# The tails of token mixing in two column tiles of TensorE instead of zero-padded weights

## The chip, the cores and the metric

The kernel runs on one core of one Trainium2 chip. The metric is the device time of one execution in microseconds (us), from five runs shown as their median, lowest and highest. A separate profiler record of one execution gives the trace. TensorE is called PE here, its weight loads PEld, VectorE DVE, ScalarE ACT, GpSimd POOL, and SyncE (which only issues transfers here) SP.

## The reference

A pooling attention feeds an MLP mixer. Sizes: 8 batches, 8 heads, 576 tokens, head width 64, so a model width of 512.

```
k_p, v_p = mean of k, v over groups of 8 tokens          # 72 pooled keys
attn     = softmax(q @ k_p.T / 8)                         # 576 x 72 a head
x        = heads of (attn @ v_p) side by side             # 576 x 512 a batch
A        = relu(x.T @ w_tok1)                             # 512 x 256
u        = x + (A @ w_tok2).T                             # token mixing, second stage
out      = u + relu(u @ w_ch1) @ w_ch2                    # channel mixing, 1536 wide
```

The change is in the second stage of token mixing, `u = x + (A @ w_tok2).T`: 256 hidden values are contracted into 576 tokens by 512 columns.

## The kernel before

**Tiling of the tokens.** A batch has 576 tokens, which is four blocks of 128 and one of 64. The block of 64 is called the tail. Two batches (2p and 2p+1) share one tail tile of 128 partitions: the even batch has partitions 0 to 63, the odd one 64 to 127. That holds for the attention's output (`xt`) and for the mixed tail (`u_tails[:, p, :]`), so four pairs make four tail blocks, and channel mixing treats these as a ninth unit of work (n = 8) after the eight batches.

**The stage that is changed.** Line 400, `u(c)`, is the second stage of token mixing for block c. For c below 4 it is two matmuls into one accumulator of `ps_one` (a pool of three accumulator banks, line 60), one for each half of the 256 hidden values. `AT` holds the 256 hidden values on partitions, in two halves m. For c = 4, called `u4`, the block belongs to two batches with different `AT`, kept in `tails[pair, half]` (line 389). The weights of the tail tokens, `w_tok2[:, m, 512:576]`, have 64 columns. They are copied into `w_tok2t`, a tile of 128 columns for each half: for the even batch the weights are in columns 0 to 63 and the rest is zero, and for the odd batch the other way round. So four full matmuls of 128 x 128 x 512 accumulate into the same 128 x 512 accumulator. The zero columns add nothing to the other batch's rows. One DVE addition (line 411) then adds `xt` and writes `u_tails`.

**Building the padded weights.** Line 614 clears `w_tok2t` on DVE at the start. Lines 129 and 130, at the end of `permute_tok2`, copy the weights into their places with two POOL instructions. Lines 127 and 128 permute `w_tok2` itself, on POOL as well. On POOL's queue the two copies stand ahead of the loads of batch 1's q and v and of `w_ch2`, and of batch 2's k and q.

**The order of work.** The schedule is written by hand: every engine does its instructions in the order in which the program emits them. `unit(n, at)` (line 590) runs the channel mixing of unit n: for each of 12 hidden blocks four matmuls (line 512) and a ReLU on ACT (line 516), then the second layer (line 534) and the stores. Between steps of it, the tables `FIRST` to `LATER` (lines 559 to 576) name steps of the next batch to be emitted (of batch n itself with `<`, of batch n+2 with `>`): attention scores (`s`, line 253), attention times values (`av`, line 344), first token mixing (`at`, line 395), second (`u`, line 410), transposes of u (`t`, line 420, with the copy at line 421), or spilling u to memory and reading it back in transposed blocks (`M`, `T`). `u4` occurs four times, for the odd batches: in unit 0 as "t1 u4 u3", in unit 2 as "u2 t0", "u4", "t1" at successive places, and in units 4 and 6 as "u0 u2 u4" at one place. The transposes `t` share a single accumulator (`pt`), so a `t` waits until the DVE copy of the one before has emptied it.

**Row tiles.** `score4` (line 253) already divides PE: its matmuls contract over 32 partitions only, and four of them, with `tile_position=(l * 32, 0)`, sit in four row groups of the array. All other matmuls of the kernel use the array whole.

Of the kernel before, what the change touches and what calls it, by code (L numbers as in the profile page):

```python
# [9 lines left out]
BF16 = mybir.dt.bfloat16  # L10
# [10 lines left out]
def kernel(  # L21
# [14 lines left out]
    nc = tc.nc  # L36
    B, H, S, D = q.shape
    P = 128
    POOL = 8
    SP = S // POOL  # L40
    BP, BR = 64, S // 64
# [10 lines left out]
    singles = ctx.enter_context(tc.tile_pool(name="singles", bufs=1))  # L52
# [11 lines left out]
    ident = singles.tile([P, P], BF16)  # L64
    w_tok1 = singles.tile([P, 6, DT], BF16)
    w_tok2 = singles.tile([P, 2, S], BF16)
    w_tok2t = singles.tile([P, 2, 2, P], BF16)
    w_ch1 = singles.tile([P, 4, DC], BF16)
    w_ch2 = singles.tile([P, NM, DM], BF16)
    f2 = singles.tile([P, 2, S], BF16)  # L70
# [35 lines left out]
    def q_pairs(a0, a1):  # L106
        return q[0, 2 * a0:2 * a1].rearrange("(a l) (p r) d -> (l p) a (r d)", l=2, r=BR)

    def load(key, b):
        if b < B:  # L110
            load_q(b) if key == "q" else load_kv(b, k if key == "k" else v, key)

    def load_tok():
        nc.gpsimd.dma_start(out=f2, in_=moe_w_tok2.rearrange("(c p) n -> p c n", p=P))
        w = moe_w_tok1.rearrange("(p r) n -> p r n", r=BR)
        for half in range(2):
            rows = slice(half * BP, (half + 1) * BP)
            nc.gpsimd.dma_start(out=w_tok1[rows, 0:4, :],
                                in_=w[:, 0:8, :].rearrange("p (c u) n -> p c u n", u=2)[:, :, half])
        for half in range(2):  # L120
            rows = slice(half * BP, (half + 1) * BP)
            nc.gpsimd.dma_start(out=w_tok1[rows, 4 + half, :], in_=w[:, 8, :])

    def permute_tok2():
        src = f2.rearrange("t m (p r) -> t m r p", r=BR)
        dst = w_tok2.rearrange("t m (r p) -> t m r p", p=BP)
        for m in range(2):
            nc.gpsimd.tensor_copy(out=dst[:, m], in_=src[:, m])
        for half in range(2):
            nc.gpsimd.tensor_copy(out=w_tok2t[:, :, half, half * BP:(half + 1) * BP], in_=w_tok2[:, :, 8 * BP:S])  # L130

    def load_ch1():
        for g in range(3):
            cols = slice(g * 512, (g + 1) * 512)
            nc.gpsimd.dma_start(out=w_ch1[:, :, cols], in_=moe_w_ch1[:, cols].rearrange("(p c) n -> p c n", c=4))

    def load_ch2(gs):
        for g in gs:
            nc.gpsimd.dma_start(out=w_ch2[:, 4 * g:4 * g + 4, :],
                                in_=moe_w_ch2[g * 512:(g + 1) * 512, :].rearrange("(c p) n -> p c n", p=P))  # L140
# [13 lines left out]
    tails = {}  # L154

    def batch_steps(b):

        par, first = b % 2, b == 0
        st = {}
# [16 lines left out]
        def late(key):  # L176
            if key not in st:
                pool, shape = {"x": (mix, [P, 4, DM]), "u": (mix, [P, 4, DM]), "uT": (mix, [P, 4, 4 * P]),
                               "AT": (att, [P, 2, DM]), "qD": (att, [P, 2, 2, S])}[key]
                st[key] = pool.tile(shape, BF16, name=key)  # L180
            return st[key]
# [218 lines left out]
        def u(c):  # L400
            def go():
                ps = ps_one.tile([P, 512], FP32, name="p1")
                if c < 4:
                    mms = [(w_tok2[:, m, c * P:(c + 1) * P], st["AT"][:, m, :]) for m in range(2)]
                    dst, x = late("u")[:, c, :], st["x"][:, c, :]
                else:
                    mms = [(w_tok2t[:, m, half, :], tails[b // 2, half][:, m, :]) for half in range(2) for m in range(2)]
                    dst, x = u_tails[:, b // 2, :], st["xt"]
                for i, (w, a) in enumerate(mms):
                    nc.tensor.matmul(out=ps, lhsT=w, rhs=a, start=(i == 0), stop=(i == len(mms) - 1))  # L410
                nc.vector.tensor_tensor(out=dst, in0=ps, in1=x, op=ALU.add)  # L411
            return go

# [165 lines left out]
    def head(s):  # L579
        if s[0] == "d":  # L580
            ps = ps_tr.tile([P, 512], FP32, name="pt")
            for _ in range(int(s[1:])):
                nc.tensor.matmul(out=ps, lhsT=warm[:, 0:P], rhs=warm, start=True, stop=True)
        elif s[0] == "c":
            a = int(s[1:])
            (nc.vector.tensor_copy if a % 2 else nc.scalar.copy)(out=loaded[0, "q"][:, a, 0:BR * D], in_=qf[:, a, :])
        else:
            batches[0][1][s]()

    def unit(n, at):  # L590
        if n + 2 < B:
            batches[n + 2][0]()
        for i, _ in enumerate(unit_steps(n, batches[n][2] if n < B else None)):
            for s in at.get(i, "").split():
                if s[0] == "l":
                    load(s[1], n + int(s[2]))
                    continue
                ahead = {"<": 0, ">": 2}.get(s[0], 1)
                s = s.lstrip("<>")
                if n + ahead < B and ((n + ahead) % 2 or s not in ("u4", "t4", "M4", "T4")):  # L600
                    batches[n + ahead][1][s]()

    with tc.manual_schedule(engines={PE, POOLE, DVE, ACT, SYNC}):
        batches = [batch_steps(b) for b in range(B)]
        nc.vector.memset(warm, 0.0)
        for a in range(2):
            nc.sync.dma_start(out=qf[:, a:a + 1, :], in_=q_pairs(a, a + 1))
        load("k", 0)
        make_identity(nc, ident)
        load("q", 0)  # L610
        load("v", 0)
        nc.vector.memset(kpz, 0.0)
        nc.vector.memset(w_tok1[:, 4:6, :], 0.0)
        nc.vector.memset(w_tok2t, 0.0)
        load_tok()
        load_ch1()
        load("k", 1)
        permute_tok2()
        load("q", 1)
        load("v", 1)  # L620
        load_ch2((0, 1, 2))
        batches[0][0]()
        for s in HEAD.split():
            head(s)
        load("k", 2)
        load("q", 2)
        batches[1][0]()
        unit(0, FIRST)
        unit(1, SECOND)
        unit(2, THIRD)  # L630
        unit(3, FOURTH)
        for n in range(4, B + 1):
            unit(n, LATER)
# [30 lines left out]
```

The softmax here doesn't subtract the row's maximum and nothing guards it: scores larger than these inputs give would overflow.

## Time and profile before

| what | value |
|---|---|
| median of five runs | 275.58 us (274.8 to 275.73) |
| profiled execution | 274.8 us |
| its span, first to last instruction | 273.0 us |
| mean granted clock of TensorE | 0.997 |
| PE busy | 264.3 us (97%) |
| DVE, ACT, POOL busy | 141.8, 110.4, 131.1 us |
| matmuls of `u4` | 16, first at 51.5 us, last at 208.8 us |

The times of matmuls need care. Matmuls are pipelined: the trace gives a 128x512 matmul 379 ns from start to end, but the next one starts before this one ends. What a matmul takes from PE's time is the distance between starts. The table of waits names the engine that released a waiting instruction; the chain of work that ended last follows the program back from its last instruction, and gives each piece the time that it added.

### The profile page before, as it was taken

What the parts mean: (1) busy time and instruction counts of PE and PEld (TensorE: products, weight loads), DVE (VectorE), ACT (ScalarE), POOL (GpSimd) and SP (SyncE); (2) the same over time, 40 slices, a digit from 0 to 9 for tenths busy, and PEclk for the clock granted to TensorE, in tenths of its full rate; (3) what the DMA queues carried; (4) which work ended last, traced back from release to release, by engine and by line L of the source; (5) the groups of instructions that cost most, each with busy time, mean ns of one, the idle gap of its engine ahead of it and who ended that gap; (6) DMA issues with size and microseconds to landing.
All of it is one profiled execution on the core that took longest, in us unless ns stands there. A gap on an engine that the chain in (4) does not pass through costs nothing.

```text
span 273.0 us, 4513 instructions
## 1 busy us (share of the span) xinstructions
PE 264.3 (97%) x1801; PEld 130.5 (48%) x1832; DVE 141.8 (52%) x280; ACT 110.4 (40%) x182; POOL 131.1 (48%) x121
## 2 busy tenths in 40 slices
PE   8999999999999999999999999999999999999994
PEld 3874444545453544444444444544454444444443
DVE  5586777763583676466267627662665061022022
ACT  2443780058207534425632483147413603703600
POOL 8695223999998990899099999300000000000000
PEclk9999999999999999999999999999999999999998
DMA  8999999990997910994399363224223624024024
GB/s 165 191 202 208 204 205 202 226 189 5 176 133 126 214 29 5 147 221 123 77 158 221 110 119 73 59 66 115 57 61 96 129 62 99 0 56 100 2 48 106
DMA packets 36838, 32.68 MB, mean 120 GB/s; under 512 B 14289, under 2 KB 30289, under 8 KB 36817
## 3 DMA queue, kind: packets, MB, share of 16 engines
q0 software_dynamic: 18672, 17.64, 41.0%
q1 hardware_dynamic: 17984, 14.62, 21.0%
q8 instruction: 14, 0.23, 0.3%
q10 hardware_dynamic: 160, 0.13, 0.2%
q14 instruction: 8, 0.06, 0.1%
HBM read 38.21 MB, written 11.80 MB: 183 GB/s over the span
## 4 chain that ended last, share of the span: by engine, by line
PE 89%; ACT 3%; DVE 2%; DMA 2%; issue 1%; POOL 0%; POOLq 0%
PE p L512 32%; PE p L534 32%; PE p L410 6%; PE p L395 6%; PE p L344 3%; PE p L260 3%; ACT ex L265 2%; DMA kr<-in_k_dram 2%; PE pt L420 1%; ACT GT L516 1%; PE p L226 1%; PE p L546 1%; PE p L204 1%; PE pt L376 1%; PE p L461 0%
## 5 line engine op out<-in xcount | busy, mean ns | idle before, releaser
L534 PE MATMUL p<-w_ch,GT 128*128 128x512 bf16 x404 | 98.9, 379 | 0.9 <-issue 0.3
L516 ACT ACTIVATE GT<-p 128x512 bf16<-128x512 f32 x108 | 63.8, 598 | 70.4 <-PE p L512 69.5
L512 PE MATMUL p<-uT,w_ch 128*128 128x512 bf16 x371 | 91.3, 379 | 0.7
L512 PEld LDWEIGHTS <-w_ch 128*128 128x128 bf16 x432 | 40.5, 98 | 47.5 <-issue 2.7
L534 PEld LDWEIGHTS <-GT 128*128 128x128 bf16 x420 | 38.0, 98 | 42.0 <-issue 3.3
L520 DVE TENSOR_TENSOR o<-p,u 128x512 f32<-128x512 f32 x32 | 21.9, 684 | 31.2 <-PE p L534 31.0
L265 ACT ACTIVATE ex<-p 72x1024 bf16<-72x1024 f32 (+1 forms) x42 | 31.7, 807 | 13.4 <-PE p L260 13.4
L147 POOL TENSOR_TENSOR t<-t 72x512 f32<-72x512 f32 x24 | 30.3, 1264 | 1.9
L411 DVE TENSOR_TENSOR u<-p,x 128x512 bf16<-128x512 f32 x32 | 21.7, 690 | 14.7 <-PE p L410 14.4
L146 POOL TENSOR_TENSOR t<-kr 72x1024 f32<-72x1024 bf16 x12 | 25.5, 2122 | 7.2 <-DMA kr<-in_k_dram 6.5
L146 POOL TENSOR_TENSOR t<-vr 72x1024 f32<-72x1024 bf16 x12 | 25.5, 2124 | 0.8
L442 DVE STREAM_TRANSPOSE uT<-v 128x512 bf16<-128x512 bf16 x16 | 10.4, 688 | 24.0 <-DMA v<-mem 24.0
L248 DVE STREAM_TRANSPOSE qD<-qb 128x576 bf16<-128x576 bf16 x28 | 20.5, 794 | 0.4 <-DMA qb<-in_q_dram 0.4
L362 DVE TENSOR_TENSOR x<-p,den 128x512 bf16<-128x512 f32 x28 | 19.4, 691 | 1.0
L410 PE MATMUL p<-AT,w_tok 128*128 128x512 bf16 x64 | 18.4, 379 | 0.2 <-ACT GT L516 0.2
L386 ACT ACTIVATE AT<-p 128x512 bf16<-128x512 f32 x7 | 4.2, 597 | 32.2 <-PE p L395 32.2
L344 PEld LDWEIGHTS <-ex 72*128 72x128 bf16 x280 | 13.0, 98 | 7.9 <-DVE x L362 0.7
L356 DVE RECIPROCAL den<-p 128x8 f32<-128x8 f32 (+1 forms) x35 | 7.1, 202 | 15.8 <-PE p L344 15.3
L395 PE MATMUL p<-x,w_tok 128*128 128x512 bf16 x56 | 14.5, 379 | 0.1
L344 PE MATMUL p<-vp,ex 72*128 72x65 bf16 x280 | 14.1, 193 | 0.4 <-ACT ex L265 0.4
L104 POOL DMA_DIRECT2D qb<-in_q_dram x7 | 5.2, 738 | 18.1 <-DVE qD L248 14.1
L260 PE MATMUL p<-qD,kD 32*72 32x512 bf16 (+1 forms) x224 | 11.3, 294 | 0.2
(105 smaller groups left out, 205.8 us busy)
## 6 DMA issues: line engine op xcount, KB each, us to landing
out_dram<-o SPq DMA_DIRECT2D x70, 128.0 KB, 2.4
kr<-in_k_dram POOLq DMA_DIRECT2D x7, 576.0 KB, 13.9
qb<-in_q_dram POOLq DMA_DIRECT2D x7, 576.0 KB, 6.3
vr<-in_v_dram POOLq DMA_DIRECT2D x7, 576.0 KB, 14.5
w_ch<-in_moe_w_ch_dram POOLq DMA_DIRECT2D x6, 512.0 KB, 13.4
mem<-u SPq DMA_DIRECT2D x8, 256.0 KB, 2.1
v<-mem SPq DMA_DIRECT2D x8, 160.0 KB, 3.7
v<-mem SPq DMA_DIRECT2D x8, 128.0 KB, 3.2
```

The lines of the kernel that those rows point to most:

```text
L146: eng.tensor_tensor(out=t4[:, 0:n], in0=t[:, hs, 0:4], in1=t[:, hs, 4:8], op=ALU.add)
L147: eng.tensor_tensor(out=t4[:, 0:n, 0:2], in0=t4[:, 0:n, 0:2], in1=t4[:, 0:n, 2:4], op=ALU.add)
L248: nc.vector.transpose(out=late("qD")[:, g, db].rearrange("m (r j u) -> m u r j", u=2, r=BR), in_=st["qraw"][:, g].rearrange("m (u r d) -> ...
L265: nc.scalar.activation(out=exv[:, a, :, gs.start:gs.stop, n0:n0 + n], in_=pss[a][0:SP, :, 0:len(gs) * n].rearrange("j l (g n) -> j l g n", ...
L344: nc.tensor.matmul(out=halves[h // 4][:, (h % 4) * (D + 1):(h % 4 + 1) * (D + 1)], lhsT=st["ex"][:, h * S + n0:h * S + n0 + P], rhs=st["vp ...
L395: nc.tensor.matmul(out=ps, lhsT=w_tok1[:, c if c < 4 else 4 + par, m * P:(m + 1) * P], rhs=st["x"][:, c, :] if c < 4 else st["xt"], start= ...
L410: nc.tensor.matmul(out=ps, lhsT=w, rhs=a, start=(i == 0), stop=(i == len(mms) - 1))
L411: nc.vector.tensor_tensor(out=dst, in0=ps, in1=x, op=ALU.add)
L512: nc.tensor.matmul(out=ps, lhsT=w_ch1[:, kk, m * P:(m + 1) * P], rhs=uT[:, kk, :], start=(kk == 0), stop=(kk == 3))
L516: nc.scalar.activation(out=GT[:, m, :], in_=ps, func=AF.Relu)
L520: nc.vector.tensor_tensor(out=o_sb, in0=ps, in1=(u_tails if n == B else st["u"])[:, c, :], op=ALU.add)
L534: nc.tensor.matmul(out=pss[c], lhsT=GT[:, m, c * P:(c + 1) * P], rhs=w_ch2[:, m, :], start=(m == 0), stop=(m == NM - 1))
```

## The change

The second stage of token mixing for the tails uses the 64 tail columns of `w_tok2` directly, and puts the two batches into two column tiles of the array, each 64 columns wide. The even batch's matmuls write partitions 0 to 63 of the accumulator and have `tile_position` (0, 0); the odd batch's write partitions 64 to 127 and have (0, 64). Their order changes from half by half to alternating halves, so that matmuls of different column tiles follow one another. There are four matmuls and four weight loads in a `u4`, as before; each load has 64 columns instead of 128. The tile `w_tok2t`, the DVE instruction that clears it and the two POOL copies that fill it are gone. The addition into `u_tails` is as it was.

```diff
-    w_tok2t = singles.tile([P, 2, 2, P], BF16)
...
         for m in range(2):
             nc.gpsimd.tensor_copy(out=dst[:, m], in_=src[:, m])
-        for half in range(2):
-            nc.gpsimd.tensor_copy(out=w_tok2t[:, :, half, half * BP:(half + 1) * BP], in_=w_tok2[:, :, 8 * BP:S])
...
                 if c < 4:
-                    mms = [(w_tok2[:, m, c * P:(c + 1) * P], st["AT"][:, m, :]) for m in range(2)]
                     dst, x = late("u")[:, c, :], st["x"][:, c, :]
+                    for m in range(2):
+                        nc.tensor.matmul(out=ps, lhsT=w_tok2[:, m, c * P:(c + 1) * P], rhs=st["AT"][:, m, :],
+                                         start=(m == 0), stop=(m == 1))
                 else:
-                    mms = [(w_tok2t[:, m, half, :], tails[b // 2, half][:, m, :]) for half in range(2) for m in range(2)]
                     dst, x = u_tails[:, b // 2, :], st["xt"]
-                for i, (w, a) in enumerate(mms):
-                    nc.tensor.matmul(out=ps, lhsT=w, rhs=a, start=(i == 0), stop=(i == len(mms) - 1))
+                    for m in range(2):
+                        for half in range(2):
+                            nc.tensor.matmul(out=ps[half * BP:(half + 1) * BP], lhsT=w_tok2[:, m, 8 * BP:S],
+                                             rhs=tails[b // 2, half][:, m, :], start=(m == 0), stop=(m == 1),
+                                             tile_position=(0, half * BP))
                 nc.vector.tensor_tensor(out=dst, in0=ps, in1=x, op=ALU.add)
...
-        nc.vector.memset(w_tok2t, 0.0)
```

## The prediction

> **What bounds the kernel now.** I read the page's busy times first, then the chain that ended last, then the groups of instructions, and after these the timeline of the four places where `u4` stands. From the page, the busy time of each engine with its share of the span, and the chain's shares by engine:
>
> ```profile
> PE 264.3 (97%) x1801; PEld 130.5 (48%) x1832; DVE 141.8 (52%) x280; ACT 110.4 (40%) x182; POOL 131.1 (48%) x121
> ...
> PE 89%; ACT 3%; DVE 2%; DMA 2%; issue 1%; POOL 0%; POOLq 0%
> ```
>
> The reader is to see that PE is nearly always at work and is 89% of the chain, while no other engine has above 3% of it. Time taken from PE is worth something here, unless the place has another limit; time taken from POOL or DVE is worth nothing by itself. The chain also gives the price of one 128x512 matmul in a stream, by these pieces in order of time (start, length, what):
>
> ```profile
> 132.59 1.29 PE p L534 x6
> 133.89 0.56 PE p L260 x8
> ...
> 152.87 1.73 PE p L512 x8
> ```
>
> Eight in 1.73 us are 0.216 us each; the 379 ns that a group's line gives is a latency, not a price. Next, the trace's answer for the tile that the change drops, `w_tok2t`:
>
> ```profile
> L410 PEld LDWEIGHTS <-w_tok2t x16: 98/98/98, 51.5 to 208.6; 128*128 128x128 bf16 x16
> L410 PE MATMUL p<-AT,w_tok2t x16: 379/379/379, 51.5 to 208.8; 128*128 128x512 bf16 x16
> L130 POOL COPY w_tok2t<-w_tok x2: 296/297/298, 18.2 to 18.4; 128x128 bf16<-128x128 bf16 x2
> L614 DVE MEMSET w_tok2t<- x1: 272/272/272, 2.6 to 2.6; 128x256 uint32 x1
> ```
>
> These sixteen matmuls are everything that can be saved on PE: 16 x 0.216 = 3.46 us, and by pairing half of it, 1.73 us, if pairing were perfect and free.
>
> **What a tiled group costs.** No matmul of the kernel is column-tiled, but `score4` is row-tiled: eight matmuls that stream 512 columns each, four row groups at once, so two rounds, which is also what the new `u4` wants (four matmuls, two at once, two rounds). PE and its weight loads around one such group, in order of time:
>
> ```profile
> 132.43 1.46 PE L534 MATMUL p<-w_ch,GT 128*128 128x512 bf16 x6
> 133.82 0.63 PE L260 MATMUL p<-qD,kD 32*72 32x512 bf16 x8
> 134.38 1.04 PE L534 MATMUL p<-w_ch,GT 128*128 128x512 bf16 x4
> ...
> 133.81 0.15 PEld L260 LDWEIGHTS <-kD 32*72 32x72 bf16 x8 [0.42 <-issue]
> 134.37 0.54 PEld L534 LDWEIGHTS <-GT 128*128 128x128 bf16 x4 [0.41 <-issue]
> ```
>
> The six matmuls before it use their slots up to 132.43 + 6 x 0.216 = 133.73, and the next plain matmul starts at 134.38. The group takes 0.65 us of PE. Two rounds are 0.43, so 0.22 us is the price of going into tiles and out again: 0.09 ahead of the first tile and 0.13 behind. The weight loads say why: inside a plain stream the next load runs under the present matmul, but here the first load of the tiles, and the first plain load after them, stand idle for 0.41 to 0.42 us and begin only together with their own matmul. The idle time has the releaser "issue", so no other engine held it. Eight loads then take 0.15 us together, so inside the tiles they are hidden.
>
> **The change, part by part.**
>
> *The four matmuls of a `u4`.* Before: 4 x 0.216 = 0.86 us. After, by the `score4` row: 0.65 us. The unknown is bounded from both sides. Best: two rounds and no switching price, 0.43 us. Worst: the two column tiles do not run at the same time, 0.86, with the switching price 0.22 on top, and each of the four loads exposed. For a load I take the 72-column loads of line 204, sixteen in 0.93 us with matmuls between, the last one lasting 0.11, so at most 0.055 us from start to start: 0.86 + 0.22 + 0.22 = 1.30 us. I take 0.65, since the row-tiled group is the nearest row: the same number of rounds, the same 512 columns, loads about as wide (72 against 64 columns). It differs in one respect that no row covers: there each tile reads its own 32 partitions, here both tiles read all 128 partitions of different operands. That is why both ends stay in the range. The saving is 0.86 - 0.65 = 0.21 us at a place, if nothing else is late there.
>
> *A rule against it.* In the stream of line 534 the weight loads, 98 ns long, run under matmuls that use all rows, and the pace stays 0.216 us. The Trainium skill, "TensorE: Matmul & The Clock Gate", section "Part 3: Packing small matmuls — row/col tiling", says that a weight load overlaps a running matmul only if its row group differs; two column tiles use the same rows. By that rule the second tile's load would wait for the first tile's matmul and the four would go one after another, which is the 0.86 + 0.22 + 0.22 case; by the row of line 534 it would not. The same section reports 2.38 times for three column tiles, which no run here shows; as an estimate, three matmuls at 0.216 us divided by it are 0.27 us a round, near the row-tiled 0.28.
>
> *What is late next at each place.* At the first, near 51.5 us, DVE is full. Its instructions there:
>
> ```profile
> 52.26 0.41 DVE L421 COPY uT<-pt 128x512 bf16<-128x512 bf16 x1
> 52.59 0.68 DVE L411 TENSOR_TENSOR u_tails<-p,xt 128x512 bf16<-128x512 f32 x1
> 53.19 0.68 DVE L411 TENSOR_TENSOR u<-p,x 128x512 bf16<-128x512 f32 x1
> 53.79 0.41 DVE L421 COPY uT<-pt 128x512 bf16<-128x512 bf16 x1
> ...
> 54.32 0.39 PE L420 MATMUL pt<-ident,u 128*128 128x128 bf16 x4
> ```
>
> DVE goes from one to the next without a pause from 51.05 us, started by work ahead of `u4`, so an earlier `u4` does not move it. The transposes `t3` need the single accumulator that the copy at 53.79 empties at 54.20. PE now comes to them at 54.32. It would come 0.21 earlier, at 54.11, and wait to about 54.22: the place keeps 0.10 us of its 0.21. At the second (100.18 us) DVE has gaps of 0.49 and 0.87 us ahead of its next two additions, and the transposes behind find their copies done. At the third (151.84) and fourth (208.18) the next user of an accumulator is line 512, which would start at 152.49 instead of 152.70; it takes over the bank of `u0`, whose addition is one of two that run from 151.61 to 152.90, so it is over by about 152.30. These three keep 0.21 each. What follows there (scores, exponentials, the copies of transposes) is released by PE and moves along with it; of the last 60 us PE is the chain almost alone.
>
> *The removed POOL copies.* Two copies, 18.20 to 18.73, are 0.53 us of POOL. Behind them on POOL's queue are the loads of batch 1's q and v, three of `w_ch2` and batch 2's k; these start up to 0.53 us sooner. Nobody on PE waits for what they bring: q's first use is DVE at 30.38, which did wait 0.36 us for it, but the scores at 32.45 come when PE has finished its stream, and q's transposed blocks that they need are over at 31.86. So the gain is nothing. The bad side: these loads then share the DMA engines sooner with batch 1's k, which lands at 27.63. That would have to be later by more than the 0.59 us between 31.86 and 32.45 to hold PE, and a start 0.53 sooner can't displace it by more than 0.53. Zero from both sides.
>
> *The removed DVE clear.* 0.27 us at 2.62. Three small clears follow, and then DVE sits 1.83 us until q arrives at 5.06. That wait covers it: zero. If the cover were gone it would be 0.27 us sooner.
>
> *The addition at line 411* is the same instruction; it waits for the last of four matmuls as before. No wait is added on any engine but PE's own way into and out of the tiles, and behind that stand only PE's next instructions, which the 0.65 contains.
>
> **Sum.** 0.10 + 3 x 0.21 = 0.73 us less. The profiled execution took 274.8 us with a span of 273.0, so it becomes 274.07 with a span of 272.27. That execution is the fastest of the five; against the median of 275.58 the forecast is 274.85.
>
> **The rivals.**
>
> A, slower: the column tiles run one after another. One mechanism, at the four groups: no second stream of 512 columns at the same time. Price by the bounds: 0.22 to 0.44 a place, so 0.9 to 1.8 us more, 276.5 to 277.4. It decides as soon as a round of two costs above (0.86 - 0.22) / 2 = 0.32 us. For it: every present row with parallel tiles reads disjoint partitions. Against it: nothing in the trace but the likeness to the row tiles.
>
> B, no change: the tiles run at once but each round's loads are exposed, since a 64-column load may take another way than a full one; two rounds at 0.055 to 0.11 are 0.11 to 0.22 us a place, which leaves 0 to 0.1. Sum 0 to 0.4 less, 275.2 to 275.6. For it: with the tiles entered, the first load already begins only with its matmul. Against: eight loads in 0.15 us.
>
> C, faster still: no price for switching. Three places give 0.43, the first stays at 0.10 because of DVE: 1.4 us less, 274.2. Against it stands each `score4` group.
>
> **How the numbers follow.** A difference of 0.2%, 0.55 us, is about what a measurement of this kernel can tell from no change. Chances: the forecast 0.59 (0.5 to 0.95 less), A 0.22, B 0.14, C 0.05. The forecast lies just beyond 0.55, so part of its own spread (about 0.06) falls within it: faster 0.59 - 0.06 + 0.05 = 0.58, same 0.14 + 0.06 = 0.20, slower 0.22. The five runs lie from 0.8 below to 0.15 above their median, so the likeliest case's own range is 274.0 to 275.3. The whole range goes down to 273.8, for C with half of that scatter, and up to 276.7, which takes in B and the near end of A.
>
> **What would show it.** Right: each `u4` has four matmuls of 128*64 shape; the distance from the last slot ahead of them to the next plain matmul is near 0.65 us; two of them start within some ns of each other; the transposes `t3` near 54 us start close behind the copy's end; the distance from the place near 100 us to the end of the span is about 0.63 us shorter. Wrong by A: starts of the four stand 0.216 us or more apart. Wrong by B: 0.75 to 0.86 us for the group. The forecast would also be wrong if batch 1's k landed over half a microsecond later than 27.6 us, or if PE's stream broke somewhere that now runs through.

## The result, and the profile after

| | before | after |
|---|---|---|
| median | 275.23 us (50 runs) | 274.58 us (30 runs) |
| ratio, 95% interval | | 0.9978, 0.9971 to 0.9985 |
| profiled execution, its span | 274.8 us, 273.0 us | 274.61 us, 272.8 us |

The kernel became faster by 0.65 us in the median, or 0.4 to 0.8 us by the interval of the ratio. The forecast was 0.73 us less. The page of the changed kernel, busy time by engine and the chain by engine:

```profile
PE 263.4 (97%) x1801; PEld 129.3 (47%) x1832; DVE 141.5 (52%) x279; ACT 110.4 (40%) x182; POOL 130.5 (48%) x119
...
PE 89%; ACT 3%; DVE 3%; DMA 2%; issue 1%; POOL 0%; POOLq 0%
```

PE has as many instructions as before and 0.9 us less of busy time; it is still nearly the whole chain. The second of the four places where `u4` stands, PE and then its weight loads, in order of time (start, length, engine, line, operation):

```profile
100.15 0.59 PE L513 MATMUL p<-uT,w_ch 128*128 128x512 bf16 x2
100.67 0.62 PE L409 MATMUL p<-AT,w_tok 128*64 128x512 bf16 x4
101.23 0.60 PE L513 MATMUL p<-uT,w_ch 128*128 128x512 bf16 x2
...
100.67 0.14 PEld L409 LDWEIGHTS <-w_tok 128*64 128x64 bf16 x4 [0.42 <-issue]
101.22 0.11 PEld L513 LDWEIGHTS <-w_ch 128*128 128x128 bf16 x2 [0.41 <-issue]
```

The two matmuls before the group have their slots up to 100.15 + 2 x 0.216 = 100.58, and the next plain one starts at 101.23. The group takes 0.65 us: 0.09 to get in, two rounds, and the rest to get out. The loads idle for 0.42 and 0.41 us with "issue" as the releaser, as they do at the row-tiled scores. The other three places have the same 0.65 us by the starts of their matmuls. Narrower stretches of the same timeline resolve the four matmuls into two pairs:

```profile
100.67 0.41 PE L409 MATMUL p<-AT,w_tok 128*64 128x512 bf16 x2
100.91 0.38 PE L409 MATMUL p<-AT,w_tok 128*64 128x512 bf16 x2
```

Two start together and two 0.24 us later. To see where the time went, I cut both executions at the start of each batch's first score group (for instance 81.94 and 107.12 us in the kernel before), and compare the pieces. The differences are taken before rounding to two digits:

| stretch | holds | before | after | difference | forecast |
|---|---|---|---|---|---|
| start to scores of batch 1 | removed clear and copies | 32.45 | 32.92 | +0.47 | 0 |
| scores of batch 1 to 2 | first `u4` | 25.57 | 25.49 | -0.07 | -0.10 |
| 2 to 3 | | 23.92 | 23.93 | +0.01 | 0 |
| 3 to 4 | second `u4` | 25.18 | 24.98 | -0.20 | -0.21 |
| 4 to 5 | | 26.70 | 26.70 | 0 | 0 |
| 5 to 6 | third `u4` | 26.88 | 26.68 | -0.20 | -0.21 |
| 6 to 7 | | 27.74 | 27.73 | -0.01 | 0 |
| 7 to the end | fourth `u4` | 84.59 | 84.39 | -0.20 | -0.21 |

The stretches without a `u4` agree within 0.01 us, so this is a sharper ruler than the runs' times. The four with one are 0.68 us shorter together. The first 33 us were 0.47 us longer in the profiled execution of the changed kernel, and the experiments ask whether that belongs to the change.

The first place, DVE, then the weight loads of the transposes `t3`, the four matmuls before them and the transposes themselves:

```profile
53.06 0.68 DVE L412 TENSOR_TENSOR u_tails<-p,xt 128x512 bf16<-128x512 f32 x1
53.66 0.68 DVE L412 TENSOR_TENSOR u<-p,x 128x512 bf16<-128x512 f32 x1
54.25 0.41 DVE L422 COPY uT<-pt 128x512 bf16<-128x512 bf16 x1
...
54.72 0.23 PEld L421 LDWEIGHTS <-u 128*128 128x128 bf16 x3 [0.22 <-issue]
...
53.72 1.03 PE L535 MATMUL p<-w_ch,GT 128*128 128x512 bf16 x4
54.72 0.38 PE L421 MATMUL pt<-ident,u 128*128 128x128 bf16 x4
```

The transposes start 0.06 us after the copy ends (54.66), and the four matmuls before them have their slots from 53.72 to 54.58: PE waits 0.14 us, which it did not do before.

### The profile page after: what moved, and what is told of

The parts are those of the page before. It is cut to its first block, busy times and chain, and to the rows that moved or that the text cites. A ratio compares the mean times of both kernels' runs of the same rounds, so it can differ in the third digit from the quotient of the medians.

```text
span 272.8 us, 4508 instructions
## 1 busy us (share of the span) xinstructions
PE 263.4 (97%) x1801; PEld 129.3 (47%) x1832; DVE 141.5 (52%) x279; ACT 110.4 (40%) x182; POOL 130.5 (48%) x119
## 4 chain that ended last, share of the span: by engine, by line
PE 89%; ACT 3%; DVE 3%; DMA 2%; issue 1%; POOL 0%; POOLq 0%
PE p L513 32%; PE p L535 32%; PE p L392 6%; PE p L403 5%; PE p L341 3%; PE p L257 3%; ACT ex L262 2%; DMA kr<-in_k_dram 2%; PE pt L421 1%; ACT GT L517 1%; PE p L223 1%; PE p L547 1%; PE p L409 1%; PE p L201 1%; PE pt L373 1%
```

## The experiments

Theory T: the whole gain is PE's, from two column tiles that run at once; the price of switching is paid once a group; DVE takes back half at the first place; the removed work on DVE and POOL is worth nothing. Its rivals stand with each run.

### One tile instead of two

```diff
-  nc.tensor.matmul(out=ps[half * BP:(half + 1) * BP], ..., start=(m == 0), stop=(m == 1), tile_position=(0, half * BP))
+  nc.tensor.matmul(out=ps[0:BP], ..., start=(m == 0 and half == 0), stop=(m == 1 and half == 1), tile_position=(0, 0))
...
+  # the addition only for partitions 0 to 63 of a tail; the others copied from x
```

> The changed kernel with all four matmuls of a u4 in the same column tile (0, 0), accumulating into partitions 0 to 63; the even batch's tail rows then hold the sum of both batches and the odd batch's are only x, copied by an extra small DVE instruction, so the tail rows of the output are not the reference's. Loads and matmuls have the same shapes (64 columns) and the same way into and out of the tiles; what is missing is the second tile. Theory T (two tiles run at once): four rounds, 1.08 us a group, so the stretches with the second, third and fourth place are 0.43 us longer each than in the changed kernel (25.40, 27.11 and 84.8 us). Rival (a matmul of 64 columns is cheaper by itself, whatever its tile): the groups stay at 0.65 us and the stretches at 24.98, 26.68 and 84.38.

There is one execution of this kernel, so only its stretches are compared. The second place, PE and weight loads:

```profile
101.23 0.59 PE L516 MATMUL p<-uT,w_ch 128*128 128x512 bf16 x2
101.75 1.05 PE L409 MATMUL p<-AT,w_tok 128*64 128x512 bf16 x4
102.73 0.39 PE L516 MATMUL p<-uT,w_ch 128*128 128x512 bf16 x1
...
101.75 0.57 PEld L409 LDWEIGHTS <-w_tok 128*64 128x64 bf16 x4 [0.42 <-issue]
```

From 101.23 + 0.43 = 101.66 to 102.73 the group takes 1.07 us, against 0.65 with two tiles; the stretches with the second, third and fourth place are 25.40, 27.10 and 84.82 us, each 0.43 more than in the changed kernel. (The first, 26.20, can't be compared: DVE has the extra copy there, and the first scores waited 0.18 us for q, of which more below.) Narrow matmuls are not cheaper by themselves. What saves is the second tile, and without it the change would lose 0.21 us a place, since the switching stays. The four loads now take 0.57 us, as the third and the fourth start only with the second and the third matmul (101.99 and 102.21); spread over two tiles they take 0.14.

### Each group twice

```diff
-                    for m in range(2):
+                    for m in (0, 1, 0, 1):
```

> The changed kernel with each column-tiled group issued twice into the same accumulator; the second time starts the sums anew, so the result is the same. It adds two rounds to a group and no way into or out of the tiles. Theory T (a round costs one slot of 0.216 us, the 0.22 us of switching is paid once a group): each group 1.08 us, so 3 x 0.43 and somewhat less at the first place, where DVE hides about 0.1: 1.6 to 1.75 us more than the changed kernel, 1.0 to 1.15 more than before. Rival (a round costs 0.32 and switching nothing): each group 1.30 us, 2.6 us more than the changed kernel.

The medians are 276.38 us and 275.52 for the kernel before on the same chip, and the ratio is 1.0024 (1.0006 to 1.0041). The second to fourth stretches are 25.41, 27.11 and 84.83 us, 0.43, 0.43 and 0.44 more than after.

```profile
101.18 0.59 PE L513 MATMUL p<-uT,w_ch 128*128 128x512 bf16 x2
101.71 1.05 PE L409 MATMUL p<-AT,w_tok 128*64 128x512 bf16 x8
102.70 0.61 PE L513 MATMUL p<-uT,w_ch 128*128 128x512 bf16 x2
```

Eight matmuls take from 101.61 to 102.70, 1.09 us, and four took 0.65. Two more rounds cost 0.44, so a round is 0.22 and what remains for switching is 0.65 - 0.43 = 0.22, the two terms of the forecast. The rival of costlier rounds and no switching falls. At the first place the transposes `t1` and `t3` start at 52.49 and 55.76, 3.27 us apart, against 2.97 after: of 0.43 only 0.30 shows, the rest goes into the wait for DVE. (The whole first stretch is 26.23, 0.74 longer. The score step at its beginning took 1.01 us to the next plain matmul instead of 0.56, as its second round waited for DVE's second transposed block of q, which accounts for the rest.)

### The tiles in turn

```diff
-                    for m in range(2):
-                        for half in range(2):
+                    for half in range(2):
+                        for m in range(2):
```

> The changed kernel with the two loops exchanged: both matmuls of the even batch's column tile, then both of the odd one's. Theory T, in which PE starts matmuls in order and two run at once only if neighbours in the queue sit in different tiles: three rounds instead of two (first alone, second with third, fourth alone), 0.87 us a group, so about 0.65 to 0.85 us more than the changed kernel and no gain over the kernel before. If the tiles ran free of the order, the group would stay at 0.65 us and the time that of the changed kernel. If the two tiles never ran at once here, the group takes 1.08 us, and the kernel is 0.6 to 0.9 us slower than before.

```profile
99.97 0.59 PE L513 MATMUL p<-uT,w_ch 128*128 128x512 bf16 x2
100.50 0.63 PE L409 MATMUL p<-AT,w_tok 128*64 128x512 bf16 x4
101.06 0.60 PE L513 MATMUL p<-uT,w_ch 128*128 128x512 bf16 x2
```

From 100.40 to 101.06 the group again takes 0.66 us, and the four stretches are 25.50, 24.98, 26.68 and 84.40 us, those of the changed kernel to within 0.01. By its run times it is at 0.9987 of the kernel before (0.9974 to 1.0000). My theory fell here: I had put down 0.87 us. In the program both matmuls of the even tile stand ahead of both of the odd one. The trace doesn't say which tile a matmul belongs to, but in one tile matmuls started 0.22 to 0.24 us apart, and here two start within 0.01 us of each other. So two rounds are only possible if a matmul of the second tile starts beside the first and overtakes the one between. The alternation that the change makes of the loops is therefore not what pairs them, at least for four matmuls.

### `u4` behind the transposes at the first place

```diff
-             40: "u2", 41: "t1 u4 u3", 42: "t2", 44: "t3", 46: "t4"}
+             40: "u2", 41: "t1 u3", 42: "t2 u4", 44: "t3", 46: "t4"}
```

> The changed kernel with u4 of the first place moved from ahead of u3 to behind the transposes t2, so that DVE's addition of the tail no longer stands ahead of the copy that t3 waits for. Theory T: the weight load of t3 no longer waits (it idled 0.22 us in the changed kernel), and the stretch from the transposes t1 to the transposes t0 of the next batch but one is 0.1 us shorter than the changed kernel's 48.17 us; the total 0.1 us less, below what can be told from the runs' times. If DVE did not hold the place, nothing changes.

The first stretch became 25.71 us, 0.22 longer than the 25.49 after. The time, 274.97 us, is at 0.9976 of before (0.9956 to 0.9995), which can't tell 0.2 us. DVE and PE there:

```profile
52.41 0.41 DVE L422 COPY uT<-pt 128x512 bf16<-128x512 bf16 x1
...
52.09 0.59 PE L535 MATMUL p<-w_ch,GT 128*128 128x512 bf16 x2
52.88 0.38 PE L421 MATMUL pt<-ident,u 128*128 128x128 bf16 x4 [0.19 <-DVE uT L422]
53.20 0.62 PE L409 MATMUL p<-AT,w_tok 128*64 128x512 bf16 x4
```

DVE does hold this place, but the cure was wrong: `u4` had been the work under which the copy of `t1` finished. Without it the transposes `t2` come too soon and wait for the same accumulator: the two matmuls before them have their slots up to 52.52, and the copy ends at 52.82. (The 0.19 in the row is only what is left after the modelled end of the last matmul.) The wait moved from `t3`, where it was 0.14 us, to `t2`, where it is 0.36; the 0.22 between them is what the stretch lost.

### `u4` beside a row-tiled score step

```diff
-             40: "u2", 41: "t1 u4 u3", 42: "t2", 44: "t3", 46: "t4"}
+             40: "u2", 41: "t1 u3", 42: "t2", 44: "t3"}
...
-    SECOND = {..., 13: "s2", 16: "av1 av0", ...
+    SECOND = {..., 13: "s2 <u4", 16: "av1 av0 <t4", ...
...
-    THIRD = {..., 18: "u4", ..., 32: "t4", ..., 38: ">s2", ...
+    THIRD = {..., 38: ">s2 u4", ..., 42: "t4", ...
```

> The changed kernel with u4 of the first two places moved behind the last score step s2 of the next batch, which is row-tiled, so that a column-tiled group follows a row-tiled one directly; the transposes t4 are moved along. If going from row tiles to column tiles costs no more than going out of them, one exit and one entry are paid instead of two of each: up to 0.22 us less at each of the two places, and the first place also gets its 0.1 back from DVE: 0.3 to 0.55 us less than the changed kernel, 0.9 to 1.1 less than before. If each change of tiling has its full price, only the 0.1 remains.

```profile
101.11 1.03 PE L513 MATMUL p<-uT,w_ch 128*128 128x512 bf16 x4
102.16 0.38 PE L421 MATMUL pt<-ident,u 128*128 128x128 bf16 x4
...
110.19 0.87 PE L257 MATMUL p<-qD,kD 32*72 32x512 bf16 x8
...
113.26 0.33 PE L257 MATMUL p<-qD,kD 32*72 32x64 bf16 x16
113.52 0.62 PE L409 MATMUL p<-AT,w_tok 128*64 128x512 bf16 x4
114.08 0.39 PE L535 MATMUL p<-w_ch,GT 128*128 128x512 bf16 x1
```

Here a `u4` takes from 113.52 to 114.08, 0.56 us. The score step before it gives over to it after 0.26 us, as it does to a plain matmul in the changed kernel, and the group has 0.09 less to pay than the 0.65 of a group alone, a little under half of what was hoped for. Yet the first two stretches together are 49.63 us against 49.42, and the third and fourth 52.00 against 51.67, so the moves lost 0.21 and 0.33 us.

At the first place the transposes `t2` wait 0.36 us for DVE as in the run above (`t3` had waited 0.14), and the scores of batch 1 waited for q by 0.09, which is not the move's doing. At the second the transposes `t1` wait 0.19 us: the slots before them end at 101.97, they start at 102.16, and the copy that empties their accumulator runs from 101.69 to 102.11. And the score step `s1` took 0.81 us to the next plain weight load at 111.00, against 0.58 in the changed kernel. The transposes `t4` no longer stand ahead of it, and its third matmul, which needs the second of the two accumulators of `s0`, started at 110.45, 0.05 after ACT had finished the exponentials of `s0` at 110.40. 0.19 and 0.23 less the 0.09 saved are the 0.33.

The time, 275.12 us, is at 0.9986 of before (0.9966 to 1.0006). It is no improvement on the changed kernel.

### The early work alone

Three runs of the changed kernel, and two kernels run twice: the changed one with the unread padded tile, its clear and its copies put back, and the kernel before without them.

```diff
+    w_tok2t = singles.tile([P, 2, 2, P], BF16)
...
+        for half in range(2):
+            nc.gpsimd.tensor_copy(out=w_tok2t[:, :, half, half * BP:(half + 1) * BP], in_=w_tok2[:, :, 8 * BP:S])
...
+        nc.vector.memset(w_tok2t, 0.0)
```

and for the kernel before, besides leaving these lines out:

```diff
-  mms = [(w_tok2t[:, m, half, :], tails[b // 2, half][:, m, :]) ...
+  mms = [(w_tok2[:, m, S - P:S], tails[b // 2, half][:, m, :]) ...
```

> The changed kernel as it is, once more, as the control for the others. Theory T (the whole gain is PE's: each u4 takes 0.65 us instead of 0.86, the first place gives half of it back to DVE): 0.61 us less than before, and each column-tiled group again 0.65 us from the last plain slot to the next plain matmul. In the profile of the changed kernel the first 25 us ran 0.46 us later than in that of the kernel before. Theory T says that this is the scatter of the first loads, so this profile may start sooner, and its span then lies nearer 272.4. Rival R (the removed clear and copies move the first loads and cost 0.46 us): the start is late by 0.46 us again, and batch 1's k lands near 29 us instead of 27.6 again.

> The changed kernel with the padded tile, its DVE clear and its two POOL copies put back, though nobody reads the tile. Theory T: the same time as the changed kernel within 0.2 us, so 0.4 to 0.8 us less than before; POOL's load of batch 1's q starts 0.53 us later again and nothing on PE moves. Rival R: the start is again as in the kernel before, so it is 0.3 to 0.5 us faster than the changed kernel, about 1.0 us less than before. A second rival (part of the gain is the removed POOL work): 0.2 to 0.5 us slower than the changed kernel.

> The kernel before without the padded tile, its clear and its copies: the four full matmuls of a u4 take the last 128 columns of w_tok2 instead, so the tail rows of the output (the last 64 tokens in the kernel's order, of every batch) are another sum than the reference's; the number and shape of the instructions on PE are those of the kernel before. This is the early part of the change alone. Theory T: the same as before within 0.2 us. Rival R: 0.3 to 0.5 us slower. The rival with a gain from POOL: 0.2 to 0.5 us faster.

> The changed kernel a third time, beside the next two on the same chip, to weigh the early work alone. If the removed clear and copies cost nothing, it stands 0.5 to 0.7 us below the kernel before. If they cost something at the start, it stands at 0.2 to 0.4 below, and the next one lower.

> The changed kernel with the unread padded tile, its clear and its copies, again. It took 0.53 us less than the repeat of the changed kernel when both ran on one chip, with intervals that overlap. If that was scatter, it is within 0.25 us of the third run of the changed kernel; if the early work matters, it is again 0.3 to 0.6 us faster.

> The kernel before with full matmuls on the last 128 columns of w_tok2 and no clear and copies, again (the tail rows of the output are another sum than the reference's). If the early work costs nothing: the time of the kernel before within 0.25 us. If its absence costs time: 0.3 to 0.6 us slower than before.

| kernel | ratio to before, 95% interval | start to scores of batch 1 |
|---|---|---|
| changed | 0.9978 (0.9971 to 0.9985) | 32.92 |
| changed, again | 0.9989 (0.9975 to 1.0004) | 33.51 |
| changed, third | 0.9980 (0.9956 to 1.0005) | 32.64 |
| changed, early work kept | 0.9969 (0.9957 to 0.9981) | 33.04 |
| the same, again | 0.9965 (0.9949 to 0.9981) | 33.44 |
| before, without early work | 1.0007 (0.9994 to 1.0021) | 32.84 |
| the same, again | 0.9989 (0.9968 to 1.0009) | 32.35 |

The changed kernel's own start lies between 32.64 and 33.51 us, and the kernels with the early work, the kernel before among them (32.45), cover the same range. So the 0.47 us of the first comparison is within the scatter of the first loads, and rival R has nothing left in this piece of the profiles. In the later stretches the kept work changes nothing: 25.50, 24.98, 26.68 and 84.38 us, all within 0.01 of after. A gain by the removed work is not seen either, as the kernels that keep it are not slower.

The scatter can reach past the first 33 us. In the second run of the kernel before without early work, the stretch with the first `u4` is 25.87 us, 0.30 longer than the 25.57 before. DVE and PE there:

```profile
31.33 2.85 DVE L245 STREAM_TRANSPOSE qD<-qb 128x576 bf16<-128x576 bf16 x4
...
32.35 0.94 PE L257 MATMUL p<-qD,kD 32*72 32x512 bf16 x8
33.23 2.33 PE L509 MATMUL p<-uT,w_ch 128*128 128x512 bf16 x10
```

DVE takes up batch 1's k at 28.80 us here, 1.17 later than before, and its transposes of q are later too. The second of them ends at 32.83, and the second round of the scores starts at 32.88, 0.52 us after the first instead of 0.24. The table of waits has no entry for this: PE counts as idle only from the modelled end of a matmul, and this wait, 0.28 us, is shorter than a matmul's 0.38. The first run of this kernel lost 0.05 us by the same wait (there q's own transfer held DVE for 0.77 us), and the runs with one tile, with the doubled group and with `u4` beside `s2` lost 0.18, 0.45 and 0.09. None of the three profiles with the early work shows it, and none of the changed kernel's three either. DVE took up k between 27.63 and 29.25 us with that work and between 28.01 and 30.11 without, so the ranges overlap, but a small cost by this way can't be excluded.

What stays open is a small cost of removing it: both runs with the work kept lie 0.1 to 0.2% below those of the changed kernel in their ratios. But the intervals overlap, in the last comparison the medians are 274.80 (kept) and 274.72 (changed), and the kernel before came out once slower and once faster without that work than with it. A few tenths of a microsecond either way can't be told here.

## Why the prediction was right

**The price of a group.** 0.65 us was taken from the row-tiled scores and 0.65 was measured. Both terms hold one by one: a round is a slot (0.22 by the doubled group), and switching costs 0.22. The open difference, that both tiles read all 128 partitions of different operands, made none; no row had shown beforehand that it wouldn't. Rival A would have cost what one tile costs, 1.07 us a group; rival B needed loads that show, and they took 0.14 us for four; rival C is refuted by the 0.22 us that each of the four groups pays.

**The rule against it.** The row of line 534 was the right one to follow. Column tiles share all rows, and their four loads went in within 0.14 us, from 100.67 to 100.81. The second round came only at 100.91, so its loads ran under the first matmuls. The Trainium skill, "TensorE: Matmul & The Clock Gate", section "Part 3: Packing small matmuls — row/col tiling", lists that a load overlaps a running matmul only where the row group differs (an earlier sentence of the section also lets a load into the background weight buffer go ahead); here they overlapped in the same row group.

**What was late next.** The first place was to keep 0.10 us because of DVE's copy ahead of `t3`; it kept 0.07, with a wait of 0.14 us where 0.11 was worked out. That DVE is the limit was also shown by the doubled group, of whose 0.43 us only 0.30 arrived. The other three places gave 0.20 each against 0.21.

**The early work.** Zero was forecast for the clear and for the copies, and the profiles with and without that work don't contradict it, within the few tenths left open. One step of that working was wrong, and that it did no harm in this execution was luck: that batch 1's k could be displaced by no more than 0.53 us, against a slack of 0.59. In the changed kernel DVE took up that k at 28.99 us instead of 27.63:

```profile
28.99 1.22 DVE L143 TENSOR_TENSOR t<-kr 72x1024 f32<-72x1024 bf16 x1 [1.90 <-DMA kr<-in_k_dram]
...
32.92 0.19 PEld L257 LDWEIGHTS <-kD 32*72 32x72 bf16 x8 [0.42 <-ACT kD L194]
```

That is 1.36 us later, of which 0.47 is the late start. The removal isn't needed for this: with the copies kept, it was taken up at 28.53 and 29.25 us in the two runs, and the changed kernel's other two runs have 28.17 and 28.27. The scores still came on PE's own time, their two rounds 0.24 us apart at 32.92 and 33.16. But DVE's second transposed block of q, which the second round needs, was ready only at 32.94, so 0.22 us were left; before, it was 0.82 (31.88 and 32.70; the 0.59 counts to the first round). With `u4` beside `s2`, k was taken up at 30.11, and then PE also waited 0.51 us for the pooled keys themselves, a wait that the prediction had not weighed. The scatter of this transfer was the quantity to bound, from more than one execution, not the shift of its neighbours alone.

**The sum.** 0.73 forecast, 0.68 by the stretches, 0.65 by the medians. That the medians come so near is in part luck: the changed kernel's repeats on two chips were 0.26 and 0.92 us below the kernel before there. The forecast of the time itself, 274.85 us, started from a median of five runs, 275.58, which fifty runs put at 275.23.

## What to carry to other kernels

A group of tiled matmuls has a fixed price for going in and out of tiles (0.22 us here) and a price a round; with only two rounds saved out of four, half of the gain goes into the switch, so tiling pays by the number of rounds saved each time. Before giving a saving its full value, look at what else runs at that place: a shorter step that had covered another engine's copy uncovers it, and moving the step away can cost more than it saves. When the difference is a quarter of a per cent, cut the execution at events that both kernels have; here the stretches that the change doesn't touch agreed to 0.01 us, apart from those that the scatter of the first loads reached.

## What the runs showed that I had not expected

The order of the four matmuls in the program didn't matter: with both matmuls of the first tile ahead of both of the second, the group still took 0.66 us, two rounds. So, as far as the starts tell, a matmul passed an earlier one that waited for its own tile. And the first loads scatter by more than the whole effect: the scores of batch 1 began between 32.35 and 33.67 us in the profiles of kernels that do the same until then, apart from one clear and two copies.
